# Block-sparse attention and top-1 experts on one core: indirect transfers moved to other steps, dense steps reordered, one more unit in the planned units' buffers

## The chip, the cores and the metric

The kernel runs on one core of one Trainium2 chip. The metric is the device time of one execution in microseconds. Three runs of the kernel before gave 632.45, 634.87 and 638.0 us; the median is 634.87. The traced execution is a fourth one.

## The reference

The input is q, k and v for 4 batches, 8 heads, 768 positions and 64 values a head. Queries and keys are in 24 blocks of 32. A query block sees its own block and both neighbours, blocks 0 and 23, and three sampled blocks; blocks 0 and 23 see all. The result, 3072 tokens of 512 values, is the input of a layer of 8 experts, of which each token takes one.

```
scores = q @ k.T / 8;  scores = where(mask, scores, -1e9)
attn = softmax(scores);  x = (attn @ v)              # as 3072 x 512
logits = x @ w_gate;  e = argmax(logits)
gate = softmax(logits)[e] * sigmoid((x @ w_output_gate)[e])
out[t] = gate * (relu(x[t] @ w1[e]) @ w2[e])         # w1 512x1024, w2 1024x512
```

## The kernel before, in words

The program is written as a list of steps. `in_order` (line 78) keeps every engine's instructions in the order of the program, so what is written first is done first on its engine, and each engine is a queue: an instruction that waits holds all behind it. That goes for SP, which issues plain transfers, and for POOL (GpSimd), which issues the indirect ones, too.

**Attention.** Two passes over batch pairs (`bp`), 26 steps each (PER): four dense elements (blocks 0 and 23, class `Dense`), then 22 sparse ones (class `Sparse`, two for each of 11 block pairs). An element passes through three steps: scores `pS` (lines 462, 526), maxima `dM` on VectorE (469, 534) and exponentials `aE` on ScalarE (477, 542) in its first, transposition `pT` of the probabilities with a copy out of PSUM (`turned`, 422 to 431) in its second, the product with V `pO` (495, 502, 556) and the division `fin` in its third. So a step holds one element's scores, the last one's transposition and the one before's product. Two PSUM banks serve all transpositions (`psT`).

A sparse pair needs K blocks copied into a ring of three (`gather_k`: one on ScalarE, five on POOL, line 392; `window_k` on VectorE), three or two steps ahead, and V rows fetched by two indirect transfers of POOL (`gather_v`, 409), one step ahead.

**Routing.** Each finished group of 128 tokens is stored to `xscr` (`store_x`, SP), turned and multiplied with the gates. Tokens are sorted in six groups (RG). `route_a`, `route_r`, `route_b`, `route_c` find each token's place, and `route_d` (735) scatters one row of 64 bytes for each of 128 tokens into `table` in DRAM, an indirect transfer of POOL. `choose` picks early units of 256 tokens of one expert, as soon as a group is sorted; five are chosen so (NE), from groups 1, 2, 2, 3 and 4.

**Experts.** The work is cut in units of two token tiles (or one), 8 chunks a unit (NFC, 128 hidden values each). Chunk n is due at step 31 + n (FIRST is 31); the numbers of chunks and steps below go by that. `load_t` reads a unit's rows of `table` (SP), `load_x` fetches the tokens' x by indirect transfers (POOL, 908), `x_t` and `x_l` turn x: either on TensorE with copies by ScalarE and VectorE (units in PEX, lines 938 to 945), or `x_s` splits it on ScalarE and VectorE (918, 919) and SP issues DMA transposes (933). `load_w` loads a chunk's weights (SP, 512 KB), `w_h` and `w_l` split them in two fp16 halves on ScalarE (966) and VectorE (970), `p_h` is the first product (984), `h_h` and `h_l` its relu (997, 1003), `p_y` the second product (1016), `y_o` the scaling (1027), and `store_y` writes the tokens' rows of the output by indirect transfers (POOL, 1033).

Units 0 to 4 are early: they use buffers of their own (`early_buffers`, two buffers of 24 KB a partition that the first pass's K and V leave), with conversions two chunks ahead. After the last group `plan_ops` (751) plans units 5 to 15 on VectorE, in chunks 26 to 29 (PLAN); from chunk 30 on `load_g` reads the plan into SP's registers. These units use the attention's buffers, with weights in a ring of 24 pieces (`piece`) and conversions three chunks ahead. Eight further units stand behind a condition and are not run with these inputs.

Within a step the order is by rank. `run(step, rank)` does the attention's and the routing's work of that rank, `mixed(step, lo, hi)` the experts'. What `at(step, 3, ...)` collects is done at the end of the step, in the order in which it was collected: K and V fetches of all pairs first, then stores, routing, scatters, `choose`, early units' table reads and x loads.

The lines that set the steps of the indirect transfers before are these:

```
at(u0 - 1, 3, gather_v, bp, i)                       # both halves
at(t0 + 5 + (t - a) // 2, 3, route_d, t)             # 18 18 19 19, 26 26 27 27, 34 34 35 35, 44 44 45 45, 50 50 51
n0 = max(t0 + 6, FIRST + 8 * u - 5)                  # 27, 35, 42, 50, 58
at(max(n0 + 1, FIRST + 8 * u - 4), 3, load_x, u)     # 28, 36, 43, 51, 59, two tiles each
do(max(t - 9, end + 1), 1, load_x, u)                # planned units, in chunks
```

## Time and profile before

| | |
|---|---|
| median of three runs | 634.87 us (632.45 to 638.0) |
| the profiled execution's own time | 641.2 us |
| its span, first to last instruction | 639.4 us |
| granted TensorE clock, mean | 0.94 |
| TensorE busy | 558.7 us, 87% of the span |
| VectorE, ScalarE, POOL busy | 390.1, 345.0, 232.5 us |
| bytes moved by DMA | 135.75 MB, 212 GB/s in the mean |
| POOL's indirect transfers | 44 V halves, 24 scatters, 28 x tiles, 28 output tiles |

The profile gives start and length of every instruction, and for an engine's idle time what ended it. "issue" means that the instruction waited for nothing that the profile knows. Busy time of TensorE is modelled from its issue. The granted clock is 1.00 at 2.4 GHz and 0.5 at 1.2 GHz. The scores of the first expert chunk's step (31) start at 182.8 us, the last element's (step 51) at 329.7 us; chunk 30 starts at 375.8 us.

### The profile page before, as it was taken

How to read it: one execution, taken by the hardware profiler on the slowest of the kernel's cores; microseconds unless marked ns; L12 is line 12 of the kernel's file. 1: busy time of each engine (PE TensorE's matmuls, PEld its weight loads, DVE VectorE, ACT ScalarE, POOL GpSimd, SP SyncE). 2: the span in 40 equal slices, each digit the busy share in tenths (PEclk: the TensorE clock that was granted, in tenths of full speed). 3: DMA queues.
4: the chain of work that ended last, by engine and by line, in shares of the span. 5: the costliest groups of instructions: out<-in, count | busy, mean ns of one | idle time of the engine just before them, and what ended most of it. 6: DMA issues, size and time to landing. Idle time of an engine off the chain costs nothing. (4 is left out here: it accounts for less than half of the span.)

```text
span 639.4 us, 18425 instructions
## 1 busy us (share of the span) xinstructions
PE 558.7 (87%) x7221; PEld 385.5 (60%) x7221; DVE 390.1 (61%) x754; ACT 345.0 (54%) x619; POOL 232.5 (36%) x347
## 2 busy tenths in 40 slices
PE   4789868998789799889989978679997999799995
PEld 3467655765466576666757645456665666466663
DVE  4457765565577477648644673556666647656780
ACT  1446645566566367537654544445575456645761
POOL 4834553526608752674340241201123023103201
PEclk8699998899999899979998999798998999799999
DMA  8959996772985697676452459799799649912300
GB/s 318 287 152 292 312 281 182 218 237 63 282 256 173 211 292 220 187 211 210 142 186 87 147 189 393 245 386 371 277 260 318 131 155 290 295 26 69 97 12 30
DMA packets 61727, 135.75 MB, mean 212 GB/s; under 512 B 23744, under 2 KB 30400, under 8 KB 61377
## 3 DMA queue, kind: packets, MB, share of 16 engines
q1 hardware_dynamic: 50048, 97.23, 49.2%
q0 software_dynamic: 11584, 37.27, 18.1%
q8 instruction: 59, 0.97, 0.6%
q14 instruction: 36, 0.29, 0.2%
HBM read 124.64 MB, written 15.60 MB: 219 GB/s over the span
## 5 line engine op out<-in xcount | busy, mean ns | idle before, releaser
L984 PE MATMUL h<-xb,kr 128*128 128x256 f16 (+1 forms) x960 | 102.7, 258 | 11.8 <-DVE hh L1003 8.9
L984 PEld LDWEIGHTS <-kr 128*128 128x128 f16 x960 | 83.1, 100 | 39.2 <-issue 12.0
L1016 PE MATMUL S<-kr,hh 128*128 128x512 f16 x390 | 99.0, 386 | 0.0
L1033 POOL DMA_INDIRECT out_dram<-yo,tab x18 | 24.8, 1378 | 157.1 <-ACT yo L1027 110.6
L469 DVE TENSOR_REDUCE mx<-S 128x4 f32<-128x1024 f32 x44 | 53.7, 1220 | 37.4 <-PE S L462 16.3
L477 ACT ACTIVATE P<-S,mx 128x256 f32<-128x256 f32 x176 | 69.3, 482 | 10.8 <-DVE mx L469 8.5
L392 POOL TENSOR_TENSOR kr<-kn,eighth 128x256 f32<-128x256 f32 x110 | 68.5, 653 | 14.0 <-PE S L462 8.2
L429 ACT COPY pt<-T 128x512 f32<-128x512 f32 x66 | 36.8, 590 | 51.3 <-PE T L426 50.2
L1016 PEld LDWEIGHTS <-hh 128*128 128x128 f16 x432 | 41.7, 100 | 34.0 <-issue 2.5
L409 POOL DMA_INDIRECT vt<-in_v_dram,vidx x44 | 43.0, 977 | 49.0 <-PE O L495 39.2
L462 PE MATMUL S<-kr,qall 64*32 64x256 f32 x1408 | 53.3, 396 | 0.4 <-issue 0.2
L997 ACT ACTIVATE hh<-h 128x512 f16<-128x512 f32 (+1 forms) x44 | 22.7, 516 | 52.5 <-PE h L984 52.5
L970 DVE SCALAR_TENSOR_TENSOR kr<-e,kr 128x1024 f16<-128x1024 f32 x38 | 45.4, 1221 | 9.2 <-ACT kr L966 9.2
L426 PE MATMUL T<-ident,P 128*128 128x128 f32 x352 | 49.3, 285 | 0.1
L495 PE MATMUL O<-vt,pt 128*32 128x65 f32 x1408 | 37.2, 225 | 12.9 <-issue 12.8
L1003 DVE SCALAR_TENSOR_TENSOR hh<-h,hh 128x512 f16<-128x512 f32 (+1 forms) x44 | 26.0, 592 | 35.2 <-ACT hh L997 33.3
L984 PEld LDWEIGHTS <-ws 128*128 128x128 f16 x384 | 38.0, 104 | 12.2 <-issue 3.6
L426 PEld LDWEIGHTS T<-ident,P 128*128 128x128 f32 x352 | 42.9, 150 | 0.7 <-DVE lsum L617 0.3
L735 POOL DMA_INDIRECT table<-vals,place x24 | 26.0, 1085 | 46.2 <-DVE vals L684 29.1
L495 PEld LDWEIGHTS O<-vt,pt 128*32 128x32 f32 x1408 | 28.3, 111 | 22.5 <-issue 19.9
L502 PE MATMUL O<-vc,pt 128*64 128x65 f32 x704 | 34.5, 237 | 7.2 <-issue 7.2
L970 DVE SCALAR_TENSOR_TENSOR ws<-e,ws 128x1024 f16<-128x1024 f32 x28 | 35.2, 1259 | 8.2 <-ACT ws L966 8.1
(301 smaller groups left out, 998.0 us busy)
## 6 DMA issues: line engine op xcount, KB each, us to landing
e<-in_wcat_dram SPq DMA_DIRECT2D x82, 512.0 KB
rk<-in_wcat_dram SPq DMA_DIRECT2D x24, 512.0 KB
vn<-in_v_dram SPq DMA_DIRECT2D x12, 520.0 KB
qall<-in_q_dram SPq DMA_DIRECT2D x24, 256.0 KB
xscr<-x SPq DMA_DIRECT2D x48, 128.0 KB
vc<-in_wcat_dram SPq DMA_DIRECT2D x12, 512.0 KB
vc<-in_v_dram SPq DMA_DIRECT2D x22, 260.0 KB
kn<-in_k_dram SPq DMA_DIRECT2D x2, 1536.0 KB
```

What stands on the lines that cost most here:

```text
L392: nc.gpsimd.tensor_tensor(r[:, slot], kn[bp][:, ds(rv, 1)].rearrange("p o n -> p (o n)"), eighth.to_broadcast([128, 256]), op=ALU.mult)
L409: nc.gpsimd.indirect_dma_start(t[:, s].rearrange("p b j w -> p (b j w)"), None, v, bass.IndirectOffsetOnAxis(ap=vidx[:, bp, i, s:s + 1], a ...
L426: nc.tensor.transpose(pt[:, 128 * c:128 * c + 128], p[:, 128 * c:128 * c + 128], ident)
L429: nc.scalar.copy(t[:, 0:w], pt[:, 0:w])
L462: nc.tensor.matmul(s[64 * h2 + 32 * qi:64 * h2 + 32 * qi + 32, b, hp], t[p, 64 * j + 32 * qi:64 * j + 32 * qi + 32], g[p, 1 - qi:3:1 + qi, ...
L469: nc.vector.tensor_reduce(mx, self.s.rearrange("p b h n -> p (b h) n"), axis=AX.X, op=ALU.max, negate=True)
L477: nc.scalar.activation(p[:, 256 * hp:256 * hp + 256], self.s[:, b, hp], AF.Exp, bias=self.mx[:, 2 * b + hp:2 * b + hp + 1])
L495: nc.tensor.matmul(o[row:row + 32, b, hp, 0:VW], self.t[b][:, col:col + 32], av[:, qi, b, 4 * h2 + 2 * hg + hp], start=b == 0 and hp == 0, ...
L502: nc.tensor.matmul(o[64 * h2:64 * h2 + 64, b, hp, 0:VW], self.t[b][:, col:col + 64], cv[:, b, 4 * h2 + 2 * hg + hp], start=False, stop=b = ...
L970: nc.vector.scalar_tensor_tensor(w[:, 1], piece(n), SW, w[:, 0], op0=ALU.mult, op1=ALU.subtract)
L984: nc.tensor.matmul(hps[n // 2][:, cols(n)], w[:, hl, 128 * c:128 * c + 128], x[:, xl, c], start=cnt == 0, stop=cnt == 11)
L1016: nc.tensor.matmul(y, a[:, k], w[:, l, 512:1024], start=n % 8 == 0 and cnt == 0, stop=n % 8 == 7 and cnt == 2)
```

## The change

Ranks 4 and 5 are added behind rank 3: K copies (`gather_k`) are done in rank 4 and V halves in rank 5, the first half one step earlier than before. Scatters, early table reads and early x loads have steps written out. An x load and an output write are now one tile each; for units 0 to 3 the two tiles' output writes stand in neighbouring chunks. All output writes are declared independent of each other, as the scatters were.

In a step that follows a dense element, the order is: scores of the present element, product of the one before, transposition of the first half of the last (copied by ScalarE), maxima of the present, transposition of the second half (copied by VectorE). Before, the transpositions came after the maxima and the exponentials of the present one, the first half copied by VectorE.

Unit 4 stays early in its choice, but uses the planned units' buffers and their distances (NOWN = 4): its weights load ten chunks ahead instead of five, and are split three chunks ahead. The planned units' pieces rotate by one unit. Unit 6 is no longer turned on TensorE, unit 5 is turned two chunks ahead of its first instead of five. The planned units' table reads stand ahead of the weight loads of their chunk, one unit a chunk, and their x loads thirteen chunks ahead instead of nine; the weights of units 5 and 6 are loaded two a chunk.

```diff
+NOWN = NE - 1
-EARLY_W = -3, 5, 5, 15, 21
+EARLY_T = 27, 36, 38, 47, 52
+EARLY_X = (28, 29), (37, 37), (39, 40), (48, 49), (53, 54)
+SCATTER = {0: (18, 19, 20, 21), 1: (26, 26, 27, 27), 2: (34, 34, 35, 36), 3: (44, 45, 46, 47), 4: (50, 51, 52)}
-PEX = tuple(range(NE + 2))
+PEX = tuple(range(NE + 1))
...
-    def gather_v(bp, i):
+    def gather_v(bp, i, s):
...
-        def pT(self):
-            self.t = [turned(f"{n}" + self.name, p, 384, ("dve", "act")[n // 2]) for n, p in enumerate(self.p)]
+        def pT(self, b):
+            if b == 0:
+                self.t = []
+            for n in (2 * b, 2 * b + 1):
+                self.t.append(turned(f"{n}" + self.name, self.p[n], 384, ("act", "dve")[b]))
...
-        if n < NFC * NE:
+        if n < NFC * NOWN:
             return early_buffers(0)[:, n % 4]
-        s, j = (n // 8 - NE) % 3, n % 8
+        s, j = (n // 8 - NOWN) % 3, n % 8
...
-    def store_y(u):
...
+    def store_y(a):
+        u, m = divmod(a, 2)
+        if m >= tiles_of(u):
+            return
+        i = nc.gpsimd.indirect_dma_start(
...
+        tc.declare_no_dep(i, group="out", reason="tokens differ")
+        tc.add_to_no_dep_group("out", i)
...
-                at(u0 - n, 3, gather_k, bp, i, kind, ns)
+                at(u0 - n, 4, gather_k, bp, i, kind, ns)
...
-            at(u0 - 1, 3, gather_v, bp, i)
+            for m in range(2):
+                at(u0 - 2 + m, 5, gather_v, bp, i, m)
...
-                        at(t0 + 5 + (t - a) // 2, 3, route_d, t)
+                        at(SCATTER[g][t - a], 3, route_d, t)
...
+                            at(EARLY_T[u], 3, load_t, u)
+                            for m in range(2):
+                                at(EARLY_X[u][m], 3, load_x, 2 * u + m)
...
-                do(max(t - 26, end), 0, load_g, u)
-                do(max(t - 18, end), 1, load_t, u)
-                do(max(t - 9, end + 1), 1, load_x, u)
-                do(max(t - 7, end + 2), 13, x_s, u)
+                later = end + u - NE
+                do(max(t - 26, later), 0, load_g, u)
+                do(max(t - 18, later), 0.5, load_t, u)
+                for m in range(2):
+                    do(max(t - 13, later + 1), 1, load_x, 2 * u + m)
+                do(max(t - 7, later + 2), 13, x_s, u)
...
+                x = max(t - 2 + m, EARLY_X[u][m] + 1 - FIRST) if u < NE else t - 2 if u in PEX else t - 5
...
+                do(t + 8 + yl + 1 + (m if u < NOWN else 0), 13, store_y, 2 * u + m)
...
+            elif u < NE:
+                do(n - 10, 0.6, load_w, n)
             else:
-                m = n - NFC * NE
-                first = end if m < 8 else (38, 38, 38, 38, 38, 38, 38, 40, 40, 40, 40, 40, 42, 42, 42, 44)[(m - 8) % 16]
-                do(max(n - 24 - lead + 1, first), 0.6, load_w, n)
+                do(max(n - 24 - lead + 1, end + u - NE, (30 + j // 2, 34 + j // 2)[u - NE] if u < NE + 2 else 0), 0.6, load_w, n)
...
+        if isinstance(last, Dense):
+            if before:
+                before.pO()
+            last.pT(0)
+            now.dM()
+            last.pT(1)
         mixed(step, 0, 7)
...
-        run(step, 3)
+        for rank in (3, 4, 5):
+            run(step, rank)
```

## Rows read from the trace of the kernel before

**Rows 1.** The page, its first part: busy time, share of the span and instructions of TensorE's products.

```profile
PE 558.7 (87%) x7221; PEld 385.5 (60%) x7221; DVE 390.1 (61%) x754; ACT 345.0 (54%) x619; POOL 232.5 (36%) x347
```

**Rows 2.** Busy time by stretch, in the attention part; a stretch is one step or two, from the start of one element's scores to that of the next. Columns: start and end, length, busy time (and instructions) of PE, PEld, DVE, ACT, POOL, granted clock, DMA share, GB/s.

```profile
105.27:114.86 9.59, 7.02 (x93) 5.19 (x92) 3.35 (x7) 3.17 (x8) 8.15 (x11) 0.68 0.87 226
114.86:118.89 4.03, 4.03 (x99) 2.92 (x98) 1.96 (x5) 2.21 (x6) 1.21 (x3) 0.91 0.20 74
206.87:218.64 11.77, 9.31 (x117) 6.29 (x116) 6.18 (x12) 3.98 (x9) 8.38 (x11) 0.86 0.47 133
218.64:226.73 8.09, 6.96 (x111) 4.80 (x110) 3.75 (x5) 4.78 (x9) 7.42 (x10) 1.00 1.01 312
226.73:240.26 13.53, 13.53 (x235) 10.04 (x234) 9.77 (x17) 8.97 (x19) 5.44 (x7) 1.00 0.98 302
266.78:278.57 11.79, 9.18 (x117) 6.29 (x116) 5.83 (x12) 3.81 (x9) 8.94 (x16) 0.86 0.76 232
278.57:289.12 10.55, 8.78 (x111) 5.85 (x110) 4.59 (x10) 4.77 (x9) 8.94 (x11) 0.84 0.60 169
289.12:302.66 13.54, 13.54 (x235) 10.04 (x234) 11.23 (x27) 8.97 (x19) 5.44 (x7) 1.00 0.74 222
319.57:326.08 6.51, 6.51 (x113) 4.60 (x112) 4.04 (x10) 4.21 (x9) 2.09 (x2) 1.00 0.81 250
326.08:337.14 11.06, 8.53 (x119) 5.98 (x117) 4.85 (x13) 4.87 (x12) 5.09 (x5) 0.86 0.37 125
```

**Rows 3.** The timeline of POOL in the second of these stretches, the first and the last of four indirect transfers. Columns: start, length, engine, line, operation, what is written and read, in brackets the idle time before it and what ended it.

```profile
208.15 1.01 POOL L735 DMA_INDIRECT table<-vals,place  x1 [0.17 <-issue]
...
212.00 0.96 POOL L409 DMA_INDIRECT vt<-in_v_dram,vidx  x1 [0.30 <-issue]
```

**Rows 4.** The timeline of TensorE at that time, products with V.

```profile
209.45 0.36 PE L502 MATMUL O<-vc,pt 128*64 128x65 f32 x5 [0.40 <-issue]
210.20 0.34 PE L502 MATMUL O<-vc,pt 128*64 128x65 f32 x4 [0.40 <-issue]
210.93 0.38 PE L502 MATMUL O<-vc,pt 128*64 128x65 f32 x5 [0.38 <-issue]
```

**Rows 5.** The timeline of POOL around a pair of indirect transfers: its second one.

```profile
64.41 0.94 POOL L409 DMA_INDIRECT vt<-in_v_dram,vidx  x1 [0.30 <-issue]
```

**Rows 6.** The timeline of TensorE there: the 32 score products of that step and of the next.

```profile
64.63 1.94 PE L462 MATMUL S<-kr,qall 64*32 64x256 f32 x32
...
69.17 1.09 PE L462 MATMUL S<-kr,qall 64*32 64x256 f32 x32
```

**Rows 7.** The waits of TensorE over the whole span (total us, times, longest), and of the third transposition's copy by ScalarE (ns: least, median, most).

```profile
PE T2d L426 <- DVE pt0d L431: 7.7, 7, 2.1
...
L429 ACT COPY pt2d<-T2d x8: 479/480/482, 24.4 to 181.6; 128x384 f32<-128x384 f32 x8
```

**Rows 8.** Busy time by stretch in the expert part, columns as in rows 2: four undisturbed chunks of a pair; then the chunks 30 to 32, 35 and 36, 43 and 44, 67 and 68, 91 to 93, and 115.

```profile
450.00:460.40 10.40, 10.40 (x74) 7.02 (x73) 6.03 (x7) 6.22 (x9) 0.99 (x1) 1.00 0.90 314
375.83:389.85 14.02, 10.89 (x64) 6.67 (x63) 6.87 (x14) 4.74 (x6) 2.79 (x3) 0.88 0.80 285
395.06:410.37 15.31, 8.44 (x46) 5.28 (x45) 5.57 (x6) 4.74 (x6) 6.44 (x6) 0.78 0.80 296
424.70:436.94 12.24, 7.87 (x41) 4.85 (x38) 8.44 (x9) 7.05 (x10) 3.38 (x3) 0.72 1.03 417
486.08:495.53 9.45, 6.18 (x34) 3.93 (x33) 7.08 (x8) 7.33 (x9) 2.14 (x2) 0.82 1.05 300
543.49:558.08 14.59, 10.26 (x53) 6.18 (x52) 8.57 (x9) 8.43 (x11) 2.87 (x2) 0.77 0.99 290
603.13:606.60 3.47, 2.12 (x17) 1.47 (x15) 2.58 (x4) 3.47 (x5) 0.00 (x0) 1.00 0.26 51
```

**Rows 9.** The timeline of SP's queue after the plan: the first six of eight weight loads of unit 5, and the table reads of units 5 and 6.

```profile
382.18 4.86 SPq L890 DMA_DIRECT2D rk<-in_wcat_dram  x6
...
389.05 0.94 SPq L882 DMA_DIRECT2D tab<-table  x2
```

**Rows 10.** The timeline of POOL: the first x load of unit 5.

```profile
397.13 0.95 POOL L908 DMA_INDIRECT xb<-xscr,tab  x1 [17.90 <-DMA e<-in_wcat_dram]
```

**Rows 11.** The timeline of TensorE where it turns x of unit 6, and the next product.

```profile
427.72 0.66 PE L938 MATMUL xgp<-ident,xb 128*128 128x128 f32 x4 [1.54 <-DVE hh L1003]
429.79 1.11 PE L938 MATMUL xgp<-ident,xb 128*128 128x128 f32 x4 [1.41 <-DVE xb L945]
432.32 2.08 PE L984 MATMUL h<-xb,kr 128*128 128x256 f16 x9 [1.41 <-DVE xb L945]
```

**Rows 12.** The timeline of POOL ahead of chunk 91: two output writes of one unit, then the second of the next x loads.

```profile
533.21 1.01 POOL L1033 DMA_INDIRECT out_dram<-yo,tab  x1 [10.39 <-ACT yo L1027]
538.42 1.91 POOL L1033 DMA_INDIRECT out_dram<-yo,tab  x1 [4.21 <-ACT hh L997]
...
542.09 0.97 POOL L908 DMA_INDIRECT xb<-xscr,tab  x1 [0.30 <-issue]
```

**Rows 13.** The timeline of ScalarE there: the split of that x.

```profile
545.84 1.06 ACT L918 ACTIVATE xb<-xb 128x1024 f16<-128x1024 f32 x1 [7.05 <-issue]
```

**Rows 14.** The page's costliest groups: a weight chunk's low half on VectorE (busy us, mean ns, idle before).

```profile
L970 DVE SCALAR_TENSOR_TENSOR kr<-e,kr 128x1024 f16<-128x1024 f32 x38 | 45.4, 1221 | 9.2 <-ACT kr L966 9.2
```

**Rows 15.** The page's transfers by issue: a weight chunk's size.

```profile
e<-in_wcat_dram SPq DMA_DIRECT2D x82, 512.0 KB
```

More of the change, by code (lines that the diff above doesn't have):

```diff
@@ L404, in window_v @@
         nc.sync.dma_start(vc[i % RC][0:64].rearrange("p b j w -> p (b j w)"), v[a:a + 64])
-    def gather_v(bp, i):
-        t = ring.tile([128, 2, 2, 8, VW], F32, tag="vt", name=f"vt{bp}_{i}", bufs=RV)
-        for s in range(2):
-            nc.gpsimd.indirect_dma_start(
-                t[:, s].rearrange("p b j w -> p (b j w)"), None, v,
-                bass.IndirectOffsetOnAxis(ap=vidx[:, bp, i, s:s + 1], axis=0))
-        vt[bp, i] = t
+    def gather_v(bp, i, s):
+        if s == 0:
+            vt[bp, i] = ring.tile([128, 2, 2, 8, VW], F32, tag="vt", name=f"vt{bp}_{i}", bufs=RV)
+        nc.gpsimd.indirect_dma_start(
+            vt[bp, i][:, s].rearrange("p b j w -> p (b j w)"), None, v,
+            bass.IndirectOffsetOnAxis(ap=vidx[:, bp, i, s:s + 1], axis=0))
     xt = {}
@@ L900, in xring, with load_x @@
         return xbuf[n]
-    def load_x(u):
-        m = tiles_of(u)
-        t = early_buffers(0)[:, 4] if u < NE else xring(u % 2)
-        xfs[u] = t[:, 0:512 * m].rearrange("p (m n) -> p m n", m=m)
+    def load_x(a):
+        u, m = divmod(a, 2)
+        n = tiles_of(u)
+        if m >= n:
+            return
+        if m == 0:
+            t = early_buffers(0)[:, 4] if u < NOWN else xring(u % 2)
+            xfs[u] = t[:, 0:512 * n].rearrange("p (m n) -> p m n", m=n)
         src = xscr[0:128 * RG[OF[u]][1]] if u < NE else xscr
-        for m in range(m):
-            nc.gpsimd.indirect_dma_start(
-                xfs[u][:, m], None, src, bass.IndirectOffsetOnAxis(ap=tabs[u][:, m, 1:2], axis=0))
+        nc.gpsimd.indirect_dma_start(
+            xfs[u][:, m], None, src, bass.IndirectOffsetOnAxis(ap=tabs[u][:, m, 1:2], axis=0))
     def x_s(u):
@@ L954, in wring @@
     def wring(n):
-        if n < NFC * NE:
+        if n < NFC * NOWN:
             r = n % 5
@@ L1155, in program @@
             t = 8 * u
+            yl = 2 if u < NOWN else 4
             if u >= NE:
-                do(max(t - 26, end), 0, load_g, u)
-                do(max(t - 18, end), 1, load_t, u)
-                do(max(t - 9, end + 1), 1, load_x, u)
-                do(max(t - 7, end + 2), 13, x_s, u)
-            yl = 2 if u < NE else 4
-            for m in range(2):
-                do(t - 2 + m if u < NE else max(t - 5, end + 3), 15, x_t, 2 * u + m)
-                do(t - 1 + m if u < NE else max(t - 5, end + 3), 3 if u < NE else 16, x_l, 2 * u + m)
-            do(t + 8 + yl, 4 if u < NE else 12, y_o, u)
-            do(t + 8 + yl + 1, 13, store_y, u)
+                later = end + u - NE
[4 more added lines that the diff above has]
+                do(max(t - 7, later + 2), 13, x_s, u)
+            for m in range(2):
+                x = max(t - 2 + m, EARLY_X[u][m] + 1 - FIRST) if u < NE else t - 2 if u in PEX else t - 5
+                do(x, 15, x_t, 2 * u + m)
+                do(x + 1 if u < NE else x, 3 if u < NE else 16, x_l, 2 * u + m)
+            do(t + 8 + yl, 4 if u < NOWN else 12, y_o, u)
+            for m in range(2):
+                do(t + 8 + yl + 1 + (m if u < NOWN else 0), 13, store_y, 2 * u + m)
         for n in range(NP):
-            e = n < NFC * NE
+            e = n < NFC * NOWN
             lead, yl = (2, 2) if e else (3, 4)
@@ L1216, in tile_kernel @@
             now.pS()
+        if isinstance(last, Dense):
[4 more added lines that the diff above has]
+            last.pT(1)
         mixed(step, 0, 7)
         run(step, 0)
-        if before:
+        if before and not isinstance(last, Dense):
             before.pO()
-        if now:
+        if now and not isinstance(last, Dense):
             now.dM()
@@ L1232, in tile_kernel @@
             now.aE()
-        if last:
+        if isinstance(last, Sparse):
             last.pT()
```

27 lines of the change are left out of this document (12 added, 15 removed).

## The prediction

> **What bounds the kernel now.** I read the page's busy shares first, then the stretches of single steps, then the timelines of POOL, PE, SP and ACT in the stretches that came out too long. TensorE is busy for 558.7 of 639.4 us [rows 1], so the kernel is bound by TensorE, and what can be won is what stops it or halves its clock. The reader is to see three kinds of stretch.
>
> In the attention part four stretches are long. One step takes 9.59 us where the next takes 4.03; two take 11.77 and 8.09 where the two after them take 13.53 together; two take 11.79 and 10.55 where the two after take 13.54; one takes 11.06 where the one ahead takes 6.51 [rows 2]. That is 5.6 + 6.3 + 8.8 + 4.6 = 25.3 us too much. In the second of them POOL issues four indirect transfers in a row, from 208.15 to 212.96 us [rows 3], and TensorE runs its PV products in bursts of four or five with pauses of 0.4 us, released by nothing that the trace knows [rows 4]. The other three hold the same picture. After a single pair (POOL at 64.41) the score products take 1.94 us instead of 1.09 [rows 5, 6].
>
> In the dense steps the third transposition waits for VectorE's copy of the first, 7.7 us over seven waits, because VectorE does the maxima of the next element ahead of it [rows 7].
>
> In the expert part a chunk of a pair takes 10.40 / 4 = 2.60 us at full clock [rows 8]. Six stretches are longer, and there the clock falls to half. Three stand where TensorE turns the gathered x of units 4, 5 and 6, three where ScalarE's split of x (line 918) stands ahead of its weight conversions.
>
> **Term A, indirect transfers spread.** The change moves the scatters to one a step, the two halves of a V gather to neighbouring steps, x loads and output writes to one tile a step early on, and puts POOL's K copies between them. Nothing is added: as many transfers, each of about 1 us of POOL. By the orders of steps in both programs, the runs of four and more disappear; POOL has at most three in a row (at steps 36 and 37: a V half and two of x, the latter with a wait for their table). Bounds: all 25.3 us go, or none. The nearest row for what stays is the pair [rows 5, 6]: 1.94 - 1.09 = 0.85 us. I leave that on seven steps, 6 us: **A = 19 us**. By the Trainium skill ("SBUF — State Buffer", Who interferes with whom) TensorE and ScalarE never wait on another engine; by that sentence POOL's transfers could not stop TensorE and A would be 0. The pauses in rows 4 speak against it, though they do not show the mechanism; it is the first rival.
>
> On POOL the K copies now stand behind scatters, choices and x loads of their step, and the scatter waits for VectorE's reciprocal. They are issued two or three steps ahead, and in undisturbed steps POOL is busy for 5.44 of 13.53 us [rows 2], so I cost this at nothing; it is the last rival. SP's table reads move to steps 36, 38, 47 and 52, where what stands behind them (weights five chunks ahead, q and V windows) has several steps of cover.
>
> **Term B, dense steps.** The last element's first two transpositions are copied by ScalarE, which is done with its exponentials by then, before the maxima; the third transposition then waits one such copy of 0.48 us [rows 7] less the second transposition. It also frees the P tiles before the next exponentials. Upper bound 7.7, lower bound 0 (the next scores need the exponentials, which now stand behind two copies). Eight waits of about 0.3 us stay, so **B = 5 us**.
>
> **Term C, the expert part.** Each excess is against 2.60 us a chunk, or idle time plus (1 - granted clock) x length [rows 8].
> - Unit 4: 14.02 - 3 x 2.60 = 6.2 us. Its x is now loaded in steps 53 and 54 instead of 59, so the wait for the load goes; the turning stays. Idle is 14.02 - 10.89 = 3.1 us; between 0 and 6.2 I take 3.5.
> - Unit 5: 15.31 - 2 x 2.60 = 10.1 us. SP issues eight weight loads from 382.18 on, and only at 389.05 the table rows [rows 9]; POOL stands 17.90 us until 397.13 for them [rows 10] (the row names a weight load, which the table rows are queued behind). The change issues the table read ahead of the weights, two of these a step, and turns x at chunk 38 instead of 35. What stays is the turning itself: in unit 6 that was three waits of 1.54, 1.41 and 1.41 us [rows 11], 4.4 in all, and two rounds of transpositions of 0.66 us and more; I keep 5 (bounds 1.4 and 7.0, unit 6's excess) and take 5.1.
> - Unit 6: 12.24 - 2 x 2.60 = 7.0 us, all of it turning on TensorE at half clock for most of it. The unit leaves the list of those (PEX) and goes through ScalarE, VectorE and DMA transposes as later units do: 7.0.
> - Stretches at 486.08, 543.49 and 603.13: 3.27 + 1.7, 4.33 + 3.4, and 1.35 us. At 533.21 POOL writes one tile of output, waits until 538.42 for the second, and only then loads x, until 543.06 [rows 12]; ScalarE stands 7.05 us until 545.84 for it, its weight conversions behind [rows 13]. The change declares the writes independent and loads x four chunks earlier: 14.0. The writes alone are 5.2 us apart in the row; the Trainium skill ("DMA: Bandwidth & Descriptors", Anatomy of one DMA) gives some 2.0 us fixed cost to such a transfer, by which the independence would be worth 2 us here. The sum does not hang on it, since the four chunks alone (10.4 us) cover the wait.
> - Against it: unit 4's conversions now begin three chunks ahead, so at chunk 29 VectorE does two low halves, 1.22 us each [rows 14], beside the rest of the plan's operations, and the plan releases everything after it: -2 us. Unit 4's own buffers free its weights from waiting for the rotation; what that gives is inside the first two points.
>
> **C = 3.5 + 5.1 + 7.0 + 14.0 - 2 = 27.6 us.** Late next is VectorE, then the bandwidth at the start of the planned units.
>
> **Sum.** 19 + 5 + 27.6 = 51.6; the profiled execution took 641.2 us, so 589.6. It stands 6.3 us above the median of 634.87. I take these 6.3 us to be more of the same waits and not to come off twice: the forecast is **590 us**. If they do come off, it is 583.
>
> **Rivals.**
> 1. The pauses belong to every indirect transfer, or come from something else in those steps, and spreading only moves them. For: the releaser is unknown, and a pair already costs 0.85 us. Against: pairs come in every second step, also in the short ones, and only the runs of four and more stop TensorE for 4 us. A = 0: 590 + 19 = 609.
> 2. The expert part finds a new wait. Units 5 to 7 now load 24 x 512 KB [rows 15] in chunks 30 to 37, 12.6 MB in 20.8 us or 605 GB/s; the highest rate in rows 8 is 417. If x of units 5 and 6 lands late again, C loses the points of units 5 and 6 and of the plan, about 12, and B may be nothing: 590 + 17 = 607. Against: half of these weights are not needed before chunk 45. With rival 1 it is about 626 to 630.
> 3. The change does not reach the end of the chain: the interleaved steps are full of TensorE work anyway, and the saved pauses come back as waits in the next step. About 635. Against: in rows 2 the neighbours run at full busy time with no debt.
> 4. Slower: POOL, in order, now waits for a table, a scatter's values or an output ahead of the K copies. A wait like that in rows 10, 17.90 us, is longer than two steps' lead (13.53) by 4.4 us, and the scores then stand. From ten such waits on (44 us) the gain over the median is gone; if all fifteen steps from 34 to 50 that hold such work did it, 66 us: 590 + 66 = 656. Against: those waits were there before, with K copies behind many of them.
>
> **Chances.** Forecast (575 to 602) 0.55, rival 1 0.18, rival 2 0.12, both together 0.06, rival 3 0.05, rival 4 0.04. The range 572 to 624 holds the first three cases, some 0.82, with A's and C's upper bounds below (590 - 6 - 6 - 3 and the 6.3 us in part). About 1%, 6.3 us, is what a measurement can tell from no change. Faster by more: 0.55 + 0.18 + 0.12 + half of 0.06 = 0.88; within: 0.03 + 0.05 = 0.08; slower: 0.04.
>
> **What would show it.** A: the steps at 105, 207, 267, 279 and 326 us take 4 to 5 and 6.7 to 7.5 us, and PV products no longer come in such bursts. B: the wait of the third transposition in the dense steps falls from 7.7 to some 2.5 us. C: no stop for a table at unit 5, no turning of unit 6 on PE, no ScalarE wait ahead of the split of x, and the granted clock at 1.00 from chunk 45 to the end. I am wrong if POOL's K copies end the waits of the score products, if stops of TensorE with no releaser stay at 20 us and more, or if weight loads end ScalarE's waits in chunks 30 to 45.

## The result, and the profile after

The changed kernel takes **613.25 us** (median of 4, 609.14 to 614.58) beside 636.43 us of the kernel before: ratio 0.9645, 95% interval 0.9567 to 0.9722. It gained 23 us; forecast were 590 us and a gain of 45. The profiled execution took 613.64 us with a span of 611.8. The page's busy time of TensorE, as in [rows 1]:

```profile
PE 545.7 (89%) x7213; PEld 377.0 (62%) x7213; DVE 384.0 (63%) x753; ACT 343.2 (56%) x618; POOL 232.7 (38%) x347
```

The span cut at the same places in both kernels, from the first scores of each step and the first product of each chunk. The last three columns are profiles of later experiments: 17 is the kernel before once more, 13 the changed one once more, 14 the changed one with two repairs (experiment 10).

| stretch, us | before | changed | exp. 17 | exp. 13 | exp. 14 |
|---|---|---|---|---|---|
| up to step 4 (first dense steps) | 39.7 | 37.4 | 35.4 | 36.6 | 36.9 |
| steps 4 to 25 | 106.0 | 102.5 | 97.7 | 101.9 | 100.0 |
| steps 26 to 31 (second dense steps) | 41.9 | 49.3 | 40.2 | 46.6 | 37.6 |
| steps 32 to 50 | 142.0 | 136.4 | 126.2 | 126.6 | 126.1 |
| step 51 to chunk 29 | 46.2 | 40.2 | 39.6 | 39.6 | 39.5 |
| chunks 30 to 47 | 68.9 | 60.9 | 71.0 | 59.3 | 51.7 |
| chunks 48 to 126 | 184.1 | 172.6 | 183.7 | 172.1 | 169.4 |
| to the end | 10.6 | 12.4 | 10.7 | 11.9 | 10.7 |

The first two columns hold the answer: nearly every stretch got shorter, the second dense steps got longer by 7.5 us, and chunks 30 to 47 gained less than they should.

Busy time by stretch of the changed kernel, columns as in [rows 2], which these answer: steps 18, 19, 35 and 36, 43 and 44, 45 and 46, and 50.

```profile
103.90:107.60 3.70, 3.70 (x93) 2.83 (x92) 3.50 (x7) 2.86 (x8) 3.10 (x5) 1.00 0.65 188
107.60:112.30 4.70, 4.36 (x103) 3.02 (x103) 2.15 (x6) 2.55 (x7) 3.91 (x6) 1.00 0.85 261
207.70:222.50 14.80, 13.94 (x227) 9.47 (x226) 8.19 (x15) 8.68 (x18) 11.51 (x14) 1.00 0.68 229
...
267.20:279.90 12.70, 12.70 (x227) 9.04 (x226) 8.87 (x21) 8.71 (x18) 9.54 (x15) 1.00 0.64 207
279.90:293.60 13.70, 13.18 (x230) 9.74 (x230) 10.37 (x26) 8.63 (x19) 12.22 (x15) 1.00 0.87 252
314.30:325.70 11.40, 9.49 (x116) 5.94 (x117) 2.86 (x5) 4.67 (x9) 6.73 (x10) 0.85 0.62 213
```

Step 18 took 9.59 and takes 3.70, steps 35 and 36 took 19.86 and take 14.80, steps 43 and 44 took 22.34 and take 12.70. Step 50 took 6.52 and takes 11.40.

The fourth long stretch of before lies in steps 50 and 51. The last two lines of [rows 2] run from the first product of chunk 18 to that of 19 and on to that of 20, not from scores to scores, so they are not set against step 50 alone. From the first scores of step 50 to the first product of chunk 20, before and after:

```profile
323.14:337.14 14.00, 11.47 (x202) 8.05 (x201) 6.08 (x14) 6.92 (x14) 6.10 (x6) 0.89 0.47 148
314.26:328.37 14.11, 12.21 (x202) 7.95 (x202) 5.46 (x13) 6.11 (x12) 6.77 (x10) 0.88 0.59 204
```

Nothing was won there: the long step moved from 51 to 50.

The timelines of POOL and TensorE in that step, as in [rows 3, 4]: six indirect transfers in a row, and the products in bursts again.

```profile
315.34 1.05 POOL L414 DMA_INDIRECT vt<-in_v_dram,vidx  x1
...
321.89 0.97 POOL L742 DMA_INDIRECT table<-vals,place  x1 [0.30 <-issue]
```

```profile
317.39 0.37 PE L506 MATMUL O<-vc,pt 128*64 128x65 f32 x5 [0.21 <-issue]
318.12 0.35 PE L506 MATMUL O<-vc,pt 128*64 128x65 f32 x4 [0.36 <-issue]
318.83 0.35 PE L506 MATMUL O<-vc,pt 128*64 128x65 f32 x5 [0.36 <-issue]
```

The second dense steps: steps 29, 30 and 31 of before, then steps 29, 30 and 31 of after.

```profile
165.30:175.10 9.80, 7.00 (x96) 4.35 (x96) 5.95 (x16) 5.04 (x10) 5.04 (x8) 0.93 1.04 261
175.10:182.80 7.70, 5.96 (x104) 3.87 (x106) 5.22 (x13) 4.47 (x9) 0.00 (x0) 0.87 1.05 335
182.80:187.60 4.80, 4.80 (x101) 3.92 (x100) 3.57 (x6) 3.42 (x7) 0.00 (x0) 1.00 0.61 158
```

```profile
163.30:173.90 10.60, 9.53 (x96) 6.03 (x100) 3.98 (x9) 4.05 (x9) 1.82 (x3) 0.71 1.03 285
173.90:182.60 8.70, 6.15 (x101) 4.16 (x102) 5.38 (x16) 4.97 (x11) 0.00 (x0) 0.84 0.50 170
182.60:189.30 6.70, 6.70 (x108) 5.12 (x111) 5.30 (x13) 3.43 (x7) 0.00 (x0) 0.70 0.26 87
```

TensorE's waits in the dense steps of the changed kernel: of the scores for the exponentials over the whole span, the same in the second pass alone, and of the third transposition, which answers to [rows 7]. In the kernel before the scores waited so once, 2.1 us, in the first pass.

```profile
PE S L530 <- ACT P01d L546: 5.1, 5, 2.1
PE S L530 <- ACT P01d L546: 2.2, 2, 1.6
PE T2d L430 <- ACT pt0d L433: 2.2, 6, 0.7
```

The longest in the second pass: the scores of the next element stand for the exponentials of the last.

```profile
163.28 3.77 PE L530 MATMUL S<-kn,qall 64*64 64x384 f32 x16 [1.63 <-ACT P01d L546]
```

And unit 6: chunks 43 to 46, chunk 47, chunk 48; the first product of chunk 48; SP's queue; and VectorE's last step on the tokens that the transposing DMAs read.

```profile
404.60:415.00 10.40, 10.40 (x73) 7.04 (x72) 6.38 (x7) 6.24 (x8) 3.24 (x2) 1.00 1.03 415
415.00:426.80 11.80, 2.79 (x19) 1.69 (x18) 4.10 (x5) 3.12 (x4) 0.99 (x1) 0.80 1.10 198
426.80:431.90 5.10, 5.09 (x19) 2.63 (x20) 0.00 (x0) 0.00 (x0) 1.65 (x2) 0.50 0.93 279
```

```profile
399.97 1.22 DVE L929 SCALAR_TENSOR_TENSOR xb<-xb,xb 128x1024 f16<-128x1024 f32 x1
403.57 4.81 SPq L897 DMA_DIRECT2D e<-in_wcat_dram  x5
...
410.53 8.43 SPq L943 DMA_TRANSPOSE xb<-xb  x2
426.81 1.44 PE L994 MATMUL h<-xb,kr 128*128 128x256 f16 x6 [9.01 <-DMA xb<-xb]
```

The tokens were ready at 401.2; SP, still passing out weight loads at 415 GB/s, came to the transposing DMAs at 410.5 and was 8.4 us in issuing the two; the wait for them ended at 426.8, with 198 GB/s on the queues in the last 11.8 us. TensorE stood 9.0 us and ran chunk 48 at the low clock.

### The profile page after: what moved, and what is told of

It reads as the page before. It is cut to its first block, busy times and chain, and to the rows that moved or that the text cites. A ratio compares the mean times of both kernels' runs of the same rounds, so it can differ in the third digit from the quotient of the medians.

```text
span 611.8 us, 18428 instructions
## 1 busy us (share of the span) xinstructions
PE 545.7 (89%) x7213; PEld 377.0 (62%) x7213; DVE 384.0 (63%) x753; ACT 343.2 (56%) x618; POOL 232.7 (38%) x347
## 5 line engine op out<-in xcount | busy, mean ns | idle before, releaser
L994 PE MATMUL h<-xb,kr 128*128 128x256 f16 (+1 forms) x1044 | 111.7, 257 | 12.7 <-DMA xb<-xb 9.0
L994 PEld LDWEIGHTS <-kr 128*128 128x128 f16 x1044 | 90.8, 98 | 41.4 <-issue 12.5
L1026 PE MATMUL S<-kr,hh 128*128 128x512 f16 x438 | 109.4, 382 | 0.0
L918 POOL DMA_INDIRECT xb<-xscr,tab x20 | 23.0, 1151 | 120.9 <-DMA tab<-table 32.8
L1026 PEld LDWEIGHTS <-hh 128*128 128x128 f16 x480 | 45.9, 98 | 37.0 <-issue 1.1
L980 DVE SCALAR_TENSOR_TENSOR kr<-e,kr 128x1024 f16<-128x1024 f32 x43 | 51.3, 1222 | 15.1 <-ACT kr L976 14.8
L433 ACT COPY pt<-T 128x512 f32<-128x512 f32 x66 | 36.6, 589 | 41.8 <-PE T L430 40.9
L414 POOL DMA_INDIRECT vt<-in_v_dram,vidx x44 | 47.2, 1072 | 28.3 <-PE O L499 22.2
L1044 POOL DMA_INDIRECT out_dram<-yo,tab x20 | 21.9, 1093 | 86.8 <-ACT yo L1037 78.5
L976 ACT ACTIVATE kr<-e 128x1024 f16<-128x1024 f32 x43 | 43.7, 1053 | 0.0
L499 PE MATMUL O<-vt,pt 128*32 128x65 f32 x1408 | 34.2, 223 | 8.0 <-issue 7.6
```

The source lines that it names most:

```text
L414: nc.gpsimd.indirect_dma_start(vt[bp, i][:, s].rearrange("p b j w -> p (b j w)"), None, v, bass.IndirectOffsetOnAxis(ap=vidx[:, bp, i, s:s ...
L433: nc.scalar.copy(t[:, 0:w], pt[:, 0:w])
L499: nc.tensor.matmul(o[row:row + 32, b, hp, 0:VW], self.t[b][:, col:col + 32], av[:, qi, b, 4 * h2 + 2 * hg + hp], start=b == 0 and hp == 0, ...
L976: nc.scalar.activation(w[:, 0], piece(n), AF.Copy, scale=SW)
L980: nc.vector.scalar_tensor_tensor(w[:, 1], piece(n), SW, w[:, 0], op0=ALU.mult, op1=ALU.subtract)
L994: nc.tensor.matmul(hps[n // 2][:, cols(n)], w[:, hl, 128 * c:128 * c + 128], x[:, xl, c], start=cnt == 0, stop=cnt == 11)
```

## Experiments

Each row of four (1 to 4, 5 to 8, 9 to 12, 13 to 16) and the last two ran beside runs of the kernel before on one chip; ratios are against those. The record numbers the chips of these five rows 5, 4, 12, 5 and 9. The kernel before took 642.5 us beside experiments 1 to 4, 639.3 beside 5 to 8, and 608.5, 608.7 and 608.5 beside the rest. So ratios are compared inside the two sorts of rows, and the changed kernel was run again in the second (13).

| experiment | us | ratio (95%) |
|---|---|---|
| 1 unit 6 on TensorE | 613.96 | 0.957 (0.948–0.966) |
| 2 unit 6 six chunks sooner | 624.95 | 0.967 (0.957–0.977) |
| 3 weights 16 chunks ahead | 605.08 | 0.947 (0.938–0.955) |
| 4 dense order in first pass only | 604.32 | 0.941 (0.935–0.948) |
| 5 output writes later | 607.43 | 0.952 (0.949–0.955) |
| 6 gathers as before | 628.65 | 0.982 (0.977–0.986) |
| 7 output writes in order | 613.37 | 0.960 (0.957–0.963) |
| 8 as 3, turned earlier | 596.69 | 0.936 (0.932–0.940) |
| 9 turned earlier, weights as changed | 583.64 | 0.960 (0.956–0.964) |
| 10 as 8 and 4 together | 573.35 | 0.943 (0.939–0.948) |
| 11 as 10, old dense order | 575.95 | 0.947 (0.943–0.951) |
| 12 as 10, step 50 spread | 573.37 | 0.943 (0.939–0.947) |
| 13 changed kernel | 596.24 | 0.980 (0.975–0.985) |
| 14 as 10 | 575.07 | 0.947 (0.943–0.952) |
| 15 as 12 | 574.51 | 0.945 (0.940–0.950) |
| 16 before, gathers alone changed | 611.55 | 1.007 (1.003–1.011) |
| 17 kernel before | 610.26 | 1.001 (0.997–1.006) |
| 18 as 12 | 576.58 | 0.948 (0.939–0.957) |

**1. Unit 6 on TensorE.**

```diff
-PEX = tuple(range(NE + 1))
+PEX = tuple(range(NE + 2))
```

> Edit: the changed kernel, with unit 6 turned by TensorE again (in the list of units that TensorE turns). Theory 1 (the missing gain stands before unit 6, whose two transposing DMAs land late): the 9.0 us stop before unit 6's first product and the half clock behind it go (chunks 47 and 48 together 16.9 us, about 5.1 usual), and TensorE gets back some 7 us of turning: net 4 to 6 us less, about 608 us. Rival (unit 6's weights are as late as its tokens): the stop stays at the same place with the weights' narrowing as its end, and the turning comes on top: 613 to 620 us.

The stop before unit 6 is gone, turning costs 2.5 us (chunk 46 takes 5.11), and a stop of the same kind stands before unit 8, the next pair that is turned by DMA:

```profile
PE h L994 <- DMA xb<-xb: 5.5, 1, 5.5
```

The place is as theory 1 has it; the price moved on, which it had not said. 608 us were expected; the ratio is 0.0075 below the changed kernel's, inside its interval.

**2. Unit 6 six chunks sooner.**

```diff
-    do(max(t - 13, later + 1), 1, load_x, 2 * u + m)
-do(max(t - 7, later + 2), 13, x_s, u)
+    do(33 if u == NE + 1 else max(t - 13, later + 1), 1, load_x, 2 * u + m)
+do(35 if u == NE + 1 else max(t - 7, later + 2), 13, x_s, u)
-    x = ... else t - 2 if u in PEX else t - 5
+    x = ... else t - 2 if u in PEX else 37 if u == NE + 1 else t - 5
```

> Edit: the changed kernel, with unit 6's tokens loaded in chunk 33, scaled in 35 and turned by DMA from chunk 37 instead of 35, 41 and 43. Theory 1 (the transposing DMAs sit behind the weight loads that were issued before them): they are six chunks sooner in line, the stop before unit 6's first product goes and nothing is added on TensorE: 10 to 12 us less, about 602 us. Rival (the transposing DMAs are slow by themselves and hold SP's line while they are issued, 4.7 and 3.6 us): the stop moves to the weights that are issued behind them: 611 to 616 us, with a weight conversion at the end of TensorE's longest wait.

A miss of mine. Unit 6's tokens are turned into the buffer of unit 4, which has two chunks left at that point: those are computed with unit 6's tokens, and TensorE waits for the transposing DMAs at chunk 37.

```profile
PE h L994 <- DMA xb<-xb: 23.1, 1, 23.1
```

It shows only that the transposing DMAs come late there too, behind the weights. Experiments 8 and 9 ask the question again.

**3. Weights 16 chunks ahead.**

```diff
-do(max(n - 24 - lead + 1, ...), 0.6, load_w, n)
+do(max(n - (24 if u < NE + 2 else 16) - lead + 1, ...), 0.6, load_w, n)
```

> Edit: the changed kernel, with the weights of unit 7 and of all later units asked for 16 chunks ahead instead of 24 (so that 16 weight loads instead of 24 are asked for in chunks 30 to 37). Theory 1: with 8 loads of 512 KB less in front (1.28 us each at the 410 GB/s of that stretch) unit 6's transposes land some 10 us sooner: 8 to 10 us less, about 604 us. Rival (the transposes' own pace or SP's order is the limit): the stop of 9.0 us stays within 2 us, 613 us; or the later weights are late for unit 8 on, then new stops with a weight conversion at their end and over 615 us.

No stop at unit 6 (theory 1), and again one before unit 8, 5.85 us. The profile puts its end down to a weight conversion on VectorE, as the second half of the rival has it (over 615 us, which did not come). SP's queue ahead of it:

```profile
423.99 0.31 SPq L897 DMA_DIRECT2D e<-in_wcat_dram  x1
432.32 0.35 SPq L889 DMA_DIRECT2D tab<-table  x1
...
437.41 8.99 SPq L943 DMA_TRANSPOSE xb<-xb  x2
```

SP stood from 424.3 to 432.3, 5.8 us of it for table buffers that output writes still read, and then came late to the transposes. Which of the two held the product, the conversion or the transposes, this run does not show; experiment 8 takes the stop away by turning earlier.

**4. New dense order in the first pass alone.**

```diff
+turns = isinstance(last, Dense) and last.k[0] == 0
-if isinstance(last, Dense):
+if turns:
```

> Edit: the changed kernel, with the new order of the dense steps (turning ahead of the maxima, first half on ScalarE) in the first of the two passes alone; the second has the old order and engines. Theory 2 (in the second pass the new order costs, since ScalarE's copies stand behind the exponentials of a step with more other work): the steps 27 to 31 go back from 42.3 to about 35 us: 6 to 8 us less, about 606 us. Rival (that stretch is longer because of the transfers that were moved into it): the steps stay at 41 to 43 us and the time at 613 us.

Steps 28, 29 and 30:

```profile
153.10:161.10 8.00, 5.41 (x81) 3.67 (x80) 4.44 (x9) 3.96 (x9) 7.36 (x11) 1.00 0.98 290
161.10:170.50 9.40, 7.86 (x93) 4.72 (x92) 5.87 (x16) 5.07 (x10) 4.27 (x6) 0.82 1.04 255
170.50:177.30 6.80, 5.06 (x101) 3.66 (x101) 5.20 (x14) 4.47 (x9) 0.00 (x0) 1.00 1.03 344
```

Steps 27 to 31 take 35.1 us instead of 42.3; theory 2 holds. The median fell by more than these 7 us (0.0231 of 636 is 15); the rest has no single place.

**5. Unit 1's output writes later.**

```diff
-do(t + 8 + yl + 1 + (m ...), 13, store_y, 2 * u + m)
+do(t + 8 + yl + 1 + (m + 3 * (u == 1) ...), 13, store_y, 2 * u + m)
```

> Edit: the changed kernel, with unit 1's two output writes three steps later (steps 53 and 54 instead of 50 and 51), so that GpSimd's run of six indirect transfers at 315 to 322 us of the changed kernel (one v gather, three table writes, two output writes) loses two. Theory 3 (TensorE pauses at a run of four or more indirect transfers one behind the other, not at each): step 50 goes from 11.4 us towards the 6.5 us that it had before the change: 4 to 6 us less, about 608 us by the before of the first runs. Rival (each transfer costs its own pause, wherever it is): the pauses move with the writes, step 50 loses at most 2 us: 612 to 613 us.

```profile
305.92 1.05 POOL L414 DMA_INDIRECT vt<-in_v_dram,vidx  x1 [0.15 <-issue]
...
311.16 1.00 POOL L1044 DMA_INDIRECT out_dram<-e,tab  x1 [0.30 <-issue]
```

Still five in a row: GpSimd had nothing to wait for and took the write three steps early. Step 50 takes 13.4 us, so as a test of the run's length it failed. The median is 8 us below the changed kernel's ratio, but not at this step.

**6. Gathers as before.**

```diff
-at(u0 - n, 4, gather_k, ...); at(u0 - 2 + m, 5, gather_v, bp, i, m)
+at(u0 - n, 3, gather_k, ...); at(u0 - 1, 3, gather_v, bp, i, m)
```

> Edit: the changed kernel, with the v gathers both in the step before their use again and all gathers in the rank that they had before (the table writes and token loads stay spread). Theory 3: the runs of four come back where two gathers meet table writes or token loads (steps 18, 35, 43, 44), 8 to 19 us more, 621 to 632 us. Rival (the table writes and token loads alone made the runs): within 3 us of the changed kernel, 610 to 616 us.

```profile
212.00:223.20 11.20, 9.08 (x117) 6.01 (x117) 6.28 (x11) 4.60 (x10) 8.39 (x10) 0.85 0.56 159
229.60:242.90 13.30, 10.68 (x117) 7.29 (x116) 5.08 (x10) 3.81 (x9) 6.73 (x9) 0.74 0.74 231
281.00:291.40 10.40, 9.08 (x123) 6.15 (x124) 5.25 (x12) 3.91 (x9) 7.86 (x15) 0.84 0.74 247
```

Steps 35, 37 and 43 (the lines) are long again; 0.017 of 636 is 11 us. The gathers carry most of term A here.

**7. Output writes in order again** (the two lines that declare them independent left out).

> Edit: the changed kernel, with the output writes ordered one behind the other again. Theory 4 (the three stops of the expert part in which the scaling of tokens waited, 486, 543 and 603 us of before, went because the output writes no longer hold GpSimd's line): stops of 1 to 4 us return at chunks 67, 91 and 115, 5 to 11 us more, 618 to 624 us. Rival (loading the tokens four chunks sooner took them away by itself): no stops there, 611 to 615 us.

Chunks 67, 91 and 115 stay at 1.96 us. The rival holds: loading x four chunks sooner did it, the independence is worth nothing at these places. It is worth something at another. Before unit 8 stands a stop that the changed kernel does not have, and chunks 63 and 64 take 10.55 us with a clock of 0.70, instead of 3.70 us:

```profile
PE h L994 <- DMA xb<-xb: 5.3, 1, 5.3
440.20 1.00 POOL L1044 DMA_INDIRECT out_dram<-yo,tab  x1 [7.68 <-DMA out_dram<-yo,tab]
```

The second output write of the pair waits 7.68 us for the first (0.30 in the changed kernel); behind it the table read, the loads of x and the transposing DMAs of unit 8 come later. The median does not show it, since this profile is shorter elsewhere (chunk 47 by 2.6 us, steps 32 to 50 by 4.2).

**8. As 3, tokens turned earlier.**

```diff
-do(max(t - 18, later), 0.5, load_t, u)
-do(max(t - 7, later + 2), 13, x_s, u)
-    x = ... else t - 2 if u in PEX else t - 5
+do(max(t - 16, later), 0.5, load_t, u)
+do(max(t - 9, later + 2), 13, x_s, u)
+    x = ... else t - 2 if u in PEX else t - 7
```

> Edit: the third experiment (weights of unit 7 and later asked for 16 chunks ahead), and from unit 6 on the tokens are scaled 9 and turned by DMA 7 chunks ahead instead of 7 and 5, with the table read 16 chunks ahead instead of 18. Theory 1 (the stops before units 6 and 8 are transposing DMAs that land late, because of what stands before them in SP's line): the stop of 5.8 us at chunk 63 of the third experiment goes with the slow clock behind it (7.8 us in all): 6 to 8 us less than that one, about 598 us. Rival (the DMA engines themselves are full there): the stop moves to a weight conversion within two units, 603 to 608 us.

Chunks 44 to 48 (the end of unit 5 and the start of unit 6) and 60 to 64 (the end of unit 7 and the start of unit 8), both without a stop:

```profile
402.22:415.24 13.02, 13.02 (x91) 8.82 (x90) 9.02 (x10) 8.65 (x11) 2.00 (x2) 1.00 0.91 318
441.34:448.57 7.23, 7.23 (x77) 5.32 (x76) 4.79 (x5) 7.03 (x10) 2.02 (x2) 1.00 1.03 359
```

From chunk 40 to 126 TensorE has no stop left. 8.4 us less than experiment 3 (6.8 by the ratios), as forecast.

**9. Turned earlier, weights 24 ahead** (the edit of 8 without that of 3).

> Edit: the changed kernel with the tokens of unit 6 and later scaled 9 and turned 7 chunks ahead and the table read 16 chunks ahead, as in the eighth experiment, but with the weights asked for 24 chunks ahead as in the changed kernel. Theory 1a (what counts is the place of the transposing DMAs in SP's line): two chunks sooner take 4 to 6 us off the stop of 9.0 us before unit 6, 606 to 610 us by the before of the first runs. Theory 1b (what counts are the bytes of weights that were asked for before them): the stop before unit 6 stays above 7 us, and 611 to 615 us.

The stop before unit 6 is 2.46 us here, 7.38 in experiment 13: 4.9 us off, as 1a has it, and not all, so the weights ahead count as well. The two profiles are 8.0 us apart, the medians 12.6; the rest I can't place.

**10. As 8 and 4 together** (both edits).

> Edit: the eighth experiment and the fourth together (weights 16 chunks ahead, tokens turned earlier, new order of the dense steps in the first pass alone). If the two causes are apart in time and each was read rightly, the gains add: 591.7 us of span less 5 to 7 us in steps 27 to 31, about 591 us for the median (ratio to before 0.92 to 0.93). Rival (what the second pass gives back is lost again before step 51, where the token loads and table writes then meet): 595 to 598 us.

The ratio expected was 0.92 to 0.93; it came out at 0.943, in a row where the kernel before takes 608 us and TensorE shows no bursts beside transfers (the table in the next section).

**11. As 10, old dense order in both passes** (the new branch never taken).

> Edit: as the tenth experiment, but with the old order of the dense steps in both passes. Theory 2 (in the first pass the new order gains the 2.3 us of steps 1 to 3, in the second it costs): 2 to 3 us more than the tenth. Rival (the order is worth nothing in the first pass, what it gains there is waited for later): within 1 us of the tenth.

The intervals overlap, so it is open. In the profiles steps 1 to 3 take 18.2 us in the old order and 19.7 in the new, which speaks against a gain in the first pass.

**12. As 10, step 50 spread.**

```diff
-4: (50, 51, 52)
+4: (49, 50, 51)
```

(and unit 1's writes five steps later)

> Edit: the tenth experiment, with the three table writes of the fifth group one step sooner (49, 50, 51) and unit 1's output writes five steps later (55 and 56), behind the token loads of unit 4 in GpSimd's line. Theory 3 (a run of four or more transfers is what stops TensorE): no run of more than three or four is left at step 50, which goes from about 13.5 to 7 or 8 us: 5 to 6 us less than the tenth. Rival (the pauses come with any transfers at that place): step 50 stays above 11 us and the time within 2 us of the tenth.

Step 50 takes 6.41 us here, but in experiments 9 to 11 as well: there was nothing to cure.

**13 to 16.**

> The changed kernel itself, as the measure for the other three of this row. Theory 3a (TensorE's pauses at runs of indirect transfers are there on some chips and not on others, as the ninth to twelfth experiments show none): where the before of this row stands at 632 to 643 us the pauses are there and the changed kernel stands at 609 to 618 us; where it stands at 604 to 612 us they are not, and the changed kernel gains less, 588 to 594 us, since the term for them (18 of the 27.6 us of the first two profiles) falls away on both sides.

> The tenth experiment again (weights 16 chunks ahead, tokens turned earlier, new order of the dense steps in the first pass alone), beside the changed kernel. Theories 1 and 2 (unit 6's late transposes 11.9 us, second dense pass 5 to 7 us): 15 to 20 us less than the changed kernel on any chip. Rival (on a chip with pauses the time comes back in the steps behind): under 12 us.

> The twelfth experiment again (as the tenth, with the fifth group's table writes one step sooner and unit 1's output writes behind the token loads of unit 4). Theory 3 (runs of four or more transfers stop TensorE on a chip that has the pauses): there 3 to 6 us less than the tenth, with step 50 near 7 us; on a chip without them within 1 us of the tenth. Rival (pauses come with each transfer): within 2 us on either.

> The kernel before, with nothing of the change but the gathers: the v gathers in two steps of the one each, and all gathers in the later ranks. Theory 3 (with pauses on the chip): steps 18, 35, 43 and 44 lose 8 to 15 us, ratio to before 0.976 to 0.988. Without pauses on the chip: within 2 us of before.

13: 596.24 us, a gain of 2.0% instead of 3.5%. The same six transfers as at 315 us above, and TensorE's products beside them:

```profile
306.21 1.05 POOL L414 DMA_INDIRECT vt<-in_v_dram,vidx  x1 [0.15 <-issue]
...
312.77 0.97 POOL L742 DMA_INDIRECT table<-vals,place  x1 [0.30 <-issue]
```

```profile
306.94 0.67 PE L499 MATMUL O<-vt,pt 128*32 128x65 f32 x32
307.54 0.69 PE L506 MATMUL O<-vc,pt 128*64 128x65 f32 x16
```

No pause. 14 is 21 us faster than 13 (15 to 20 expected), and 15 equals 14. 16: the gathers alone cost 0.7%.

**17 and 18.**

> The kernel before itself, for its profile beside its times. Theory 3a (the pauses at runs of transfers are a matter of the chip, not of the kernel): if its median is 604 to 612 us, steps 18, 35, 43 and 44 take 4 to 7 us instead of 9.6 to 11.8 and no run of four transfers has a pause on TensorE; if it is 632 to 643 us they take 9 to 12 us again. Rival (the missing 28 us of the faster chip are elsewhere, in transfers or in the clock): with 604 to 612 us the four steps are still above 9 us.

> The twelfth experiment a third time, for a chip with pauses if this one has them: there 3 to 6 us less than the tenth would take (15 to 20 us below the changed kernel's 0.9645 of before), a ratio to before of 0.92 to 0.935 and step 50 near 7 us; on a chip without pauses the 0.945 again.

In the kernel before, steps 35 and 36, then 43 and 44, as in [rows 2]:

```profile
191.70:204.40 12.70, 12.70 (x229) 9.05 (x228) 8.38 (x15) 8.70 (x18) 8.17 (x10) 1.00 0.42 124
...
247.60:260.20 12.60, 12.60 (x227) 9.00 (x226) 9.66 (x21) 8.65 (x17) 9.92 (x15) 1.00 0.85 265
```

19.86 and 22.34 us in the first profile; full busy time here, with four transfers in a row at 247.2 to 253.0 us. 18 met no pauses either, so the kernel with both repairs was never measured with them; 8 was, with the new dense order still in both passes.

## Why the prediction was right and wrong

The sign held, and 613 lies in the range; the gain was half of the forecast. Two steps failed, and two smaller ones beside them.

**Term C, "Unit 6: ... goes through ScalarE, VectorE and DMA transposes as later units do: 7.0."** The turning did leave TensorE (7.0 us, as priced). The new path was costed at nothing, and it cost 9.2 us of stop and 2.7 us of low clock: 11.9 against 7.0. Nor was the 7.0 all turning, as the prediction has it: turned on TensorE again, at its later place (experiment 1), the unit costs 2.5 us. The prediction counted the weight loads of chunks 30 to 37 in its second rival, but looked there for late weights and late x, and never set the two transposing DMAs in SP's line behind them. Experiments 1, 3, 8 and 9 show it: the stop goes when the unit is turned on TensorE or when fewer weights stand ahead, and shrinks from 7.4 to 2.5 us when the transposes alone stand earlier. Whether the time goes in SP's line or in the DMA engines behind it is not separated. Rival 2 named the place, x of unit 6 late, and nothing from B, and gave 607 us; the 609 us of rival 1 are nearer, by luck, since in this pair A came out in full.

**Term B, "Upper bound 7.7, lower bound 0".** The wait that it was read from went as said, from 7.7 to 2.2 us over the span. But in the second dense steps ScalarE's exponentials, now behind its two copies, became the wait of the next scores (1.63 us above), TensorE idles 7.9 us instead of 6.7, and the low clock costs 6.8 us instead of 1.7 ((1 - granted clock) x length, steps 27 to 31). In this pair of profiles B was 2.3 us gained in the first pass and 7.4 lost in the second. The loss stands in every profile (38.2 to 42.4 us in the new order, 31.4 to 35.1 in the old); the gain does not: steps 1 to 3 of this pair take 20.1 us instead of 22.4, but 19.5 instead of 18.2 in experiments 13 and 17. The text had named that very wait and still put the lower bound at 0; the bound excluded a loss without a reason. Experiments 4, 10 and 14 show that the order in the second pass is the cause (35.1, 31.6 and 31.6 us for steps 27 to 31); that it acts through this wait is read from the trace.

**Term A** came out near its price in the first pair of profiles: step 18 5.9, 35 and 36 5.1, 43 and 44 9.7, and steps 50 and 51 together 0.1 lost, in all 20.6 where 19 was forecast. Its count of "at most three in a row" failed: GpSimd took the V half, the two output writes and the three scatters of steps 49 to 52 one behind the other, with no K copy left to stand between them, so the fourth place gave nothing. What no step of mine had was that the pauses are not in every run. Runs of indirect transfers, between 185 and 345 us, against TensorE's pauses without a releaser from the start of the run until 1.5 us after it, counted from the traces (a run: starts less than 1.7 us apart; a pause: more than 0.15 us; experiment 2 left out):

```
transfers in a row        1          2          3          4 to 6
rows with before at 635 to 643 us (9 profiles)
  runs / with a pause   83 / 16    89 / 22    13 / 6     13 / 13
  mean pause, us         0.06       0.14       0.61       2.4
rows with before at 608 us (10 profiles)
  runs / with a pause  118 / 0    114 / 0     21 / 0     14 / 0
```

The bursts, two or more such pauses close together, are in all nine profiles of the first sort and in none of the ten of the second, from 30 us on. Ahead of 185 us both sorts have single stops without a releaser of 1 to 4.5 us besides, some of them with no transfer near. Where there are bursts, the first half of rival 1 is refuted: single transfers hardly have a pause, each run of four or more does. Its second half, something else in those steps, stands open, since the same runs have none in the second sort. Where there are none, A is worth nothing (steps 32 to 50 take 126.2 us in 17 and 126.6 in 13; 16: +0.7%), and between the profiles of 17 and 13 the change gains 23 us in chunks 30 to 126 and gives back 12 ahead of them. The sentence of the Trainium skill ("SBUF — State Buffer", Who interferes with whom) by which TensorE waits for nobody agrees with the second rows; the bursts of the first speak against it, without showing the mechanism. What decides between them the runs do not show. That the expectations speak of chips was a guess, and the record speaks against it: if its number names one chip, chip 5 had the kernel before at 642.5 us in the row of experiment 1 and at 608.7 in that of 13.

**The rest of C.** Unit 4 gave 3.0 us (3.5 forecast), unit 5 7.1 (5.1), the three stops before the split of x 13.8 (14.0), the plan cost nothing (2). That these stops would go by loading sooner was right; the independence of the writes is worth nothing at them, and 5.3 us of stop before unit 8 (experiment 7). In the last of the six stretches that the prediction reads the clock had not fallen: 1.00 in [rows 8].

Measured: 20.6 (A) - 5.1 (B) + 3.0 + 7.1 + 7.0 - 11.9 + 13.8 (C, 19.0) = 34.5; all other steps together lost 6.9, most of it at steps 38 and 39 (13.1 to 18.2 us), and 27.6 is the difference of the spans, where the sum had 51.6. At step 38 TensorE waits 2.1 us for x of unit 1: the last scatter of its group, its table read and its loads each stand a step later than before. The prediction asked what stands behind that table read, not who waits for the x, and put it at nothing. The kernel before waits for the same x in experiment 17 (2.5 us in step 37), and steps 37 to 39 take 23.6 us there and 24.1 in 13, so the loss is not in every pair.

**The signs.** Steps 105, 267 and 279 came short, 207 and 326 nearly. The bursts were to disappear and moved to steps 39 and 50. The clock was to stay at 1.00 from chunk 45 on; it did but for chunks 47 to 49. TensorE's stops without a releaser fell from 24.1 to 16.0 us, below the 20 that were to refute the prediction, and no weight load ends a wait of ScalarE in chunks 30 to 45. Rival 4 had no sign: no step's scores waited for a K copy. Rival 3 may stand behind part of the 6.9 us; no run separates it.

**The version to keep** is that of experiments 12, 15 and 18: the old dense order in the second pass, weights 16 chunks ahead, tokens scaled 9 and turned 7 chunks ahead, step 50 spread. It takes 574.5 us beside 596.2 of the changed kernel and 608.7 of the one before. Its new order in the first pass (11) and its spread step 50 (15 against 14) are not shown to be worth anything.

## What to carry to other kernels

A piece of work that moves from an engine to a DMA has a place in a queue: before its old cost is booked as gain, list what stands ahead of it in that queue at that time, and how long the queue's engine takes to issue it. A bound of 0 on the losing side needs a reason, above all where the text itself names who will wait. And a gain that rests on stops without a releaser is only worth what a second profile, taken in another row of runs, still shows of them.

## What was unexpected of the hardware

- Two transposing DMAs of 128 x 1024 f16 kept SP for 8.43 us and ended TensorE's wait 16.3 us after the first was issued, with 198 GB/s on all queues in the last 11.8 us. The Trainium skill ("DMA: Bandwidth & Descriptors", Latency and other measured facts) gives transposing DMAs 261 GB/s where the middle dimension is not contiguous, and more where it is; by that figure the 512 KB would take an estimated 2.0 us.
- The same program takes 635 to 643 us in some rows of runs and 608 us in others. Between its two profiles (639.4 and 604.4 us) 15.8 us lie in steps 32 to 50, 6.6 from step 51 to chunk 29, 8.4 in steps 4 to 25 and 4.3 ahead of them; the bursts of TensorE are there in the first and gone in the second, beside indirect transfers of GpSimd with a median of 0.99 us in both.
